# Decode attention with a gated MLP: w_in loaded first, and narrower streams in the last V group and the output projections

## Chip, cores and metric

One core of one Trainium2 chip. The metric is the device time of one execution in microseconds (us). A kernel's profile is one execution; its span, from the first to the last instruction, is about 2.0 us shorter than the measured time. In the names of groups, PE is TensorE's matrix multiply and PEld its weight load; DVE is VectorE, ACT is ScalarE, SP is the engine that issues the loads. In the tiles' names, uT is the vector that the gated MLP hands to w_out, and oa the attention output that goes to wo.

## The reference, cut to what matters

```python
q = x @ wq                      # x: [1, 1024], 32 heads of 128
k, v = k_cache, v_cache         # 4 groups x 65536 keys x 128, bf16; 8 heads share a group
a = softmax(q k^T / sqrt(128)) v @ wo
z = gelu(x @ w_in)              # w_in: [1024, 3584]
z1, z2 = halves of z;  z2 = layernorm(z2)
b = (z1 * (w_sp * z2 + b_sp)) @ w_out
out = g * a + (1 - g) * b       # g = sigmoid(sum(x * gate_w))
```

Everything is read once: 134 MB of K and V, 8.4 MB each of wq and wo, 7.3 MB of w_in, 3.7 MB of w_out, together 162.0 MB.

## The kernel before

All big loads go through one function into five buffers of 4 MB. SP issues them in program order, and each one waits until the buffer of the load five places earlier has been consumed.

```python
WO_SPLIT = (16, 8, 4, 2, 2)     # rows of wo for each partition, by load
W, WL = 64, 128
kv = ctx.enter_context(tc.tile_pool(name="kv", bufs=NKV))      # NKV = 5
def load(src, shape, name):
    t = kv.tile([P, CT * P], BF16, name=name, tag="kv")
    ...
    nc.sync.dma_start(out=v, in_=src)
```

The order is: wq and q; K of the four groups (each 128x128 block is transposed on PE, copied, and used as the stationary operand of the scores), with V of the group before interleaved; then w_in (z), alternating with the last group's V; then w_out and wo.

```python
# V: 8 columns are needed; the stream is padded to wv columns
wv = W if g + 1 < G else WL
nc.tensor.matmul(o_ps[g][:, o0:o0 + wv], lhsT=vt[:, c, :], rhs=scT[g][:, lo:hi, :]..., ...)
...
z_part(0); last_v(0); z_part(1); ...gelu, layernorm...; last_v(1..3)
...
# projections: one column is needed; it is broadcast to WL columns, NB = 4 to a tile, so there are two tiles
NB = 512 // WL
out_ps = [pss.tile([P, NB, WL], FP32, ...) for _ in range(NJ // NB)]
def project(src, n, vec, c0, name, first=False, last=False):
    w = load(src, (n, D), name)
    for c in range(n):
        for j in range(NJ):     # NJ = 8
            nc.tensor.matmul(out_ps[j // NB][:, j % NB, :], lhsT=w[:, c, j * P:(j + 1) * P],
                rhs=vec[:, c0 + c:c0 + c + 1].to_broadcast([P, WL]), ...)
project(w_out ...)              # 14 rows: 112 matmuls
for n in WO_SPLIT: project(wo_view[:, c0:c0 + n, :], n, oa, ...)   # 32 rows: 256 matmuls
# epilogue: copy out_ps, transpose, cast, store
```

Of the kernel before, what the change touches and what calls it, by code (L numbers as in the profile page):

```python
# [7 lines left out]
FP32 = mybir.dt.float32  # L8
BF16 = mybir.dt.bfloat16
I32 = mybir.dt.int32  # L10
ACT = mybir.ActivationFunctionType
ALU = mybir.AluOpType
AX = mybir.AxisListType

P = 128
# [3 lines left out]
CPS = 64  # L19
LAG = 4  # L20
EVAC_PAT = "vav"
WO_SPLIT = (16, 8, 4, 2, 2)
SW = 256
W = 64
WL = 128


@with_exitstack
def kernel(
# [15 lines left out]
    nc = tc.nc  # L45

    _, _, D = A_x.shape
    _, G, S, DH = A_k_cache.shape
# [3 lines left out]
    F = B_w_in.shape[1]  # L52
    FH = F // 2
    KC = D // P
    FC = FH // P
    OC = HD // P
    NJ = D // P
    QD = P // H
    NCG = S // P
    NT = NCG // CT  # L60
    SCALE = float(DH) ** -0.5
    assert DH == P and D % P == 0 and FH % P == 0 and P % H == 0
    assert S % (P * CT) == 0 and CT % CPS == 0 and CPS % TG == 0 and sum(WO_SPLIT) == OC

    const = ctx.enter_context(tc.tile_pool(name="const", bufs=1))
    wk = ctx.enter_context(tc.tile_pool(name="wk", bufs=2))
# [4 lines left out]
    pss = ctx.enter_context(tc.tile_pool(name="pss", bufs=2, space=bass.MemoryType.PSUM))  # L71
    psm = ctx.enter_context(tc.tile_pool(name="psm", bufs=1, space=bass.MemoryType.PSUM))
# [3 lines left out]
    def load(src, shape, name):  # L76
        t = kv.tile([P, CT * P], BF16, name=name, tag="kv")
        n = 1
        for s in shape:
            n *= s  # L80
        v = t[:, :n]
        if len(shape) == 2:
            v = v.rearrange("p (a b) -> p a b", b=shape[1])
        nc.sync.dma_start(out=v, in_=src)  # L84
        return v

    def load_kv(src, g, j, name):
# [9 lines left out]
    nc.scalar.dma_start(out=wb[:, 0:1], in_=B_w_sp)  # L97
    nc.scalar.dma_start(out=wb[:, 1:2], in_=B_b_sp.unsqueeze(0))

    wq_view = A_wq.rearrange("(p c) n -> p c n", c=KC)  # L100
    KH = KC // 2
    wq_t = [load(wq_view[:, i * KH:(i + 1) * KH, :], (KH, HD), "wq_t") for i in range(2)]


# [8 lines left out]
    ones_f = const.tile([P, P], FP32, name="ones_f")  # L113
# [4 lines left out]
                            op0=ALU.bitwise_and)  # L118
    nc.vector.tensor_scalar(out=pbits[:, 1:2], in0=pidx[:], scalar1=OC - 1, scalar2=None,
                            op0=ALU.bitwise_and)  # L120
    nc.vector.tensor_scalar(out=pbits[:, 2:3], in0=pidx[:], scalar1=OC.bit_length() - 1,
                            scalar2=None, op0=ALU.logical_shift_right)
# [4 lines left out]
    def one_hot(shape, dtype, in0, col, name):  # L127
# [17 lines left out]
                     start=True, stop=True)  # L145
    xm = const.tile([P, 2, KC, P // KC], FP32, name="xm")
    for t in range(2):
        nc.vector.tensor_tensor(
            out=xm[:, t], in0=xb_ps[:, t * P:(t + 1) * P].rearrange("p (i c) -> p c i", c=KC),
            in1=sel_i[:].unsqueeze(1).to_broadcast([P, KC, P // KC]), op=ALU.mult)  # L150
    xa = const.tile([P, 2, KC], FP32, name="xa")
    nc.vector.tensor_reduce(out=xa[:], in_=xm[:], axis=AX.X, op=ALU.add)
    xT = const.tile([P, KC], BF16, name="xT")
# [14 lines left out]
                            op0=ALU.add)  # L168
    nc.vector.reciprocal(out=gw[:, 2:3], in_=gw[:, 1:2])
    nc.vector.tensor_scalar(out=gw[:, 5:6], in0=gw[:, 2:3], scalar1=-1.0, scalar2=1.0,  # L170
                            op0=ALU.mult, op1=ALU.add)
    gate, wsp, bsp, gate1 = gw[:, 2:3], gw[:, 3:4], gw[:, 4:5], gw[:, 5:6]


    q_ps = psm.tile([P, H], FP32, name="q_ps", tag="m")
    for c in range(KC):
        w = wq_t[c // KH]
        for h in range(H):
            nc.tensor.matmul(  # L179
                q_ps[:, h:h + 1], lhsT=w[:, c % KH, h * DH:(h + 1) * DH], rhs=xT[:, c:c + 1],  # L180
                start=(c == 0 and h == 0), stop=(c == KC - 1), skip_group_check=True,
# [9 lines left out]
    scT, mxr, spt, o_ps, s_ps = {}, {}, {}, {}, {}  # L191
# [84 lines left out]
    def v_units(g, j, vt):  # L276
        wv = W if g + 1 < G else WL
        wc = wv // REP
# [53 lines left out]
    while steps:  # L332
        run_step()


    win_view = B_w_in.rearrange("(p c) n -> p c n", c=KC)
    zw = 512 // (2 * FC)
    z_ps = psm.tile([P, 2 * FC, zw], FP32, name="z_ps", tag="m")

    def z_part(i):  # L340
        t = load(win_view[:, i * KH:(i + 1) * KH, :], (KH, F), "win_t")
        for c in range(KH):
            w = t[:, c, :].rearrange("p (h m f) -> p h f m", h=2, f=FC)
            for hf in range(2):
                for f in range(FC):
                    nc.tensor.matmul(  # L346
                        z_ps[:, hf * FC + f, :], lhsT=w[:, hf, f, :],
                        rhs=xT[:, i * KH + c:i * KH + c + 1].to_broadcast([P, zw]),
                        start=(i == 0 and c == 0 and hf == 0 and f == 0),
                        stop=(i == 1 and c == KH - 1), skip_group_check=True)  # L350

    def last_v(j):
        rest(v_units(G - 1, j, load_kv(A_v_cache, G - 1, j, "vt")))

    z_part(0)
    last_v(0)
    z_part(1)
    z = wk.tile([P, 2 * FC], FP32, name="z")
    nc.vector.tensor_copy(out=z[:], in_=z_ps[:, :, 0])  # L359
    gt = wk.tile([P, 2 * FC], FP32, name="gt")  # L360
    nc.vector.tensor_tensor(out=gt[:], in0=z[:], in1=z[:], op=ALU.mult)
    nc.vector.tensor_scalar(out=gt[:], in0=gt[:], scalar1=0.044715, scalar2=1.0,
                            op0=ALU.mult, op1=ALU.add)
    nc.vector.tensor_tensor(out=gt[:], in0=gt[:], in1=z[:], op=ALU.mult)
    th = wk.tile([P, 2 * FC], FP32, name="th")
    nc.scalar.activation(out=th[:], in_=gt[:], func=ACT.Tanh, scale=0.7978845608028654)
    nc.vector.tensor_scalar(out=th[:], in0=th[:], scalar1=0.5, scalar2=0.5,
                            op0=ALU.mult, op1=ALU.add)
    zg = wk.tile([P, 2 * FC], FP32, name="zg")
    nc.vector.tensor_tensor(out=zg[:], in0=z[:], in1=th[:], op=ALU.mult)  # L370
    z2 = zg[:, FC:2 * FC]
    z2sq = wk.tile([P, FC], FP32, name="z2sq")
    nc.vector.tensor_tensor(out=z2sq[:], in0=z2, in1=z2, op=ALU.mult)
    rs = wk.tile([P, 2], FP32, name="rs")
    nc.vector.reduce_sum(out=rs[:, 0:1], in_=z2, axis=AX.X)
    nc.vector.reduce_sum(out=rs[:, 1:2], in_=z2sq[:], axis=AX.X)
    tot_ps = psm.tile([P, 2], FP32, name="tot_ps", tag="m")
    nc.tensor.matmul(tot_ps[:], lhsT=ones_f[:], rhs=rs[:], start=True, stop=True)
    stat = wk.tile([P, 8], FP32, name="stat")
    nc.vector.tensor_scalar(out=stat[:, 0:2], in0=tot_ps[:], scalar1=1.0 / float(FH),  # L380
                            scalar2=None, op0=ALU.mult)
    nc.vector.tensor_tensor(out=stat[:, 2:3], in0=stat[:, 0:1], in1=stat[:, 0:1], op=ALU.mult)
    nc.vector.tensor_tensor(out=stat[:, 3:4], in0=stat[:, 1:2], in1=stat[:, 2:3],
                            op=ALU.subtract)
    nc.vector.tensor_scalar(out=stat[:, 4:5], in0=stat[:, 3:4], scalar1=1e-5, scalar2=None,
                            op0=ALU.add)
    nc.scalar.activation(out=stat[:, 5:6], in_=stat[:, 4:5], func=ACT.Sqrt)
    nc.vector.reciprocal(out=stat[:, 6:7], in_=stat[:, 5:6])
    z2n = wk.tile([P, FC], FP32, name="z2n")
    nc.vector.tensor_scalar(out=z2n[:], in0=z2, scalar1=stat[:, 0:1], scalar2=stat[:, 6:7],  # L390
                            op0=ALU.subtract, op1=ALU.mult)
    nc.vector.tensor_scalar(out=z2n[:], in0=z2n[:], scalar1=wsp, scalar2=bsp,
                            op0=ALU.mult, op1=ALU.add)
    uT = const.tile([P, FC], BF16, name="uT")
    nc.vector.scalar_tensor_tensor(out=uT[:], in0=zg[:, 0:FC], scalar=gate1, in1=z2n[:],
                                   op0=ALU.mult, op1=ALU.mult)
    for j in range(1, NT):
        last_v(j)


    NB = 512 // WL
    out_ps = [pss.tile([P, NB, WL], FP32, name="out_ps", tag="spt") for _ in range(NJ // NB)]

    def project(src, n, vec, c0, name, first=False, last=False):
        w = load(src, (n, D), name)
        for c in range(n):
            for j in range(NJ):
                nc.tensor.matmul(  # L408
                    out_ps[j // NB][:, j % NB, :], lhsT=w[:, c, j * P:(j + 1) * P],
                    rhs=vec[:, c0 + c:c0 + c + 1].to_broadcast([P, WL]),  # L410
                    start=(first and c == 0 and j % NB == 0), stop=(last and c == n - 1),
                    skip_group_check=True)


# [2 lines left out]
                     rhs=ones_f[0:1, 0:1], start=True, stop=True, skip_group_check=True)  # L417
    nc.tensor.matmul(om_ps[:, :OC], lhsT=lm[:].rearrange("p h q -> p (h q)"), rhs=sel_c[:],
                     start=False, stop=True, skip_group_check=True)
# [4 lines left out]
                            op0=ALU.mult, op1=ALU.mult)  # L424
# [3 lines left out]
    c0 = 0  # L428
    for n in WO_SPLIT:
        project(wo_view[:, c0:c0 + n, :], n, oa, c0, "wo_t", last=(c0 + n == OC))  # L430
        c0 += n
    out_sb = const.tile([P, NJ], FP32, name="out_sb")
    for i, t in enumerate(out_ps):
        nc.vector.tensor_copy(out=out_sb[:, i * NB:(i + 1) * NB], in_=t[:, :, 0])  # L434
    outT_ps = psm.tile([NJ, P], FP32, name="outT_ps", tag="m")
    nc.tensor.transpose(outT_ps[:], out_sb[:], ident_f[:])
    outT = const.tile([NJ, P], BF16, name="outT")
# [4 lines left out]
    last = {}  # L442
# [37 lines left out]
```

## Time and profile before

| | before |
|---|---|
| time, median of 4 runs (before the prediction: 3 runs, 398.57) | 398.07 us (397.54 to 399.08) |
| span of the profiled run | 396.6 us |
| DMA rate over 20 to 370 us | 408 to 444 GB/s |
| first wo piece: landed; PE starts it | 377.9; 378.6 us |
| last wo piece landed; last projection matmul | 387.7; 393.6 us |

First the forty-slice view of the kernel before. Each digit is the busy share of a fortieth of the span in tenths; PEclk is the granted TensorE clock, DMA the busy share of the 16 DMA engines.

```profile
PE   0435999778788787878888688896987789799997
...
PEclk9999999999999999999999999999999977789999
DMA  8999999999999999999999999999999999999960
GB/s 357 435 423 421 425 444 433 431 423 422 428 423 408 426 414 438 426 421 416 428 440 433 431 423 422 433 425 440 433 419 430 428 431 428 438 433 423 416 259 7
```

The DMA engines are full from the second slice to the thirty-eighth. PE is full in slices 36 to 39, and it still works in the last two, when the DMA ends.

The same end by windows. The columns are the window, its length, busy time (and instruction count) of PE, PEld, DVE, ACT and POOL, then PEclk, DMA share and GB/s.

```profile
core 0: us, PE busy (x) PEld busy (x) DVE busy (x) ACT busy (x) POOL busy (x), PEclk, DMA share, GB/s
360.00:370.00 10.00, 10.00 (x178) 9.94 (x176) 0.00 (x0) 0.00 (x0) 0.00 (x0) 1.00 1.00 429
375.00:380.00 5.00, 5.00 (x90) 5.00 (x88) 0.00 (x0) 0.00 (x0) 0.00 (x0) 1.00 0.83 337
380.00:385.00 5.00, 5.00 (x91) 5.00 (x89) 0.00 (x0) 0.00 (x0) 0.00 (x0) 1.00 0.63 248
385.00:390.00 5.00, 5.00 (x90) 5.00 (x88) 0.00 (x0) 0.00 (x0) 0.00 (x0) 1.00 0.19 74
```

From 375 us on the DMA share falls while PE is busy all the time. A share of 0.63, then 0.19, is not a queue that ends at once: some of the sixteen engines end long before others. The landing events of this trace show it: a big load has sixteen of them (I read each as one engine's part), and of the last wo piece eight come by 382.3 us and eight from 386.0 to 387.7.

The timeline of the tail (start and duration in us, engine, source line, operation, output and inputs, count):

```profile
370.84 8.32 SPq L84 DMA_DIRECT2D wo_t<-in_A_wo_dram  x2
...
372.17 6.63 PE L408 MATMUL out_ps<-uT,wout_t 128*128 128x128 bf16 x112
...
378.63 14.96 PE L408 MATMUL out_ps<-oa,wo_t 128*128 128x128 bf16 x256
393.40 0.39 DVE L434 COPY out_sb<-out_ps 128x4 f32<-128x4 f32 x2 [20.52 <-PE out_ps L408]
...
394.47 0.36 SPq L439 DMA_DIRECT2D out_dram<-outT  x1
```

The 112 matmuls of w_out take 6.6 us and the 256 of wo 15.0 us, 58 ns each. The loads of wo and their time to landing:

```profile
L84 SPq DMA_DIRECT2D wo_t<-in_A_wo_dram x5: 327/328/334, 344.0 to 378.8; - x5
DMA to landing us min/median/max: 8.9/21.4/33.9
```

The median is the mean of the two ends, so two of the five landings are known; I read them as those of the first and the last piece. The first was issued at 344.0 and landed 33.9 us later, at 377.9; the last was issued at 378.8 and landed 8.9 us later, at 387.7. PE ends 5.9 us after that. The chain that ended last says the same by shares of the span: the first line by engine, the second by line of the program.

```profile
PE 71%; DMA 13%; issue 11%; ACT 3%; DVE 1%; SPq 0%; ACTq 0%
PE tps L264 27%; PE o_ps L297 18%; PE spt L243 14%; DMA kn<-in_A_k_cache_dram 13%; PE out_ps L408 5%; PE z_ps L346 3%; PE o_ps L286 2%; ACT ktt L267 1%; ACT scT L230 1%; ACT scT L249 1%; PE nb_ps L221 0%; DVE mxr L206 0%; DVE mxr L251 0%; SPq L84 0%; DVE mx L209 0%
```

### The profile page before, as it was taken

Reading aid. Unit: us, or ns where it says so; the run is one execution under the profiler, and the core shown is the slowest. Engines: PE = TensorE matmul, PEld = TensorE weight load, DVE = VectorE, ACT = ScalarE, POOL = GpSimd, SP = SyncE. Lnnn points to the kernel's source line nnn. Section 1 sums busy time; section 2 is a strip of 40 time slices with the busy share of each in tenths; the row PEclk is TensorE's granted clock in tenths of the full one; section 3 lists DMA queues with packets and bytes.
Section 4 is the critical chain, followed back from the end, with each engine's and each line's share of the span. In section 5 each row is a group of like instructions: output and inputs, shape, how many; then the busy total and the mean of one; then the engine's idle time right before and its main releaser. Section 6 shows DMA issues by size and latency. Waiting matters only on the chain.

```text
span 396.6 us, 14958 instructions
## 1 busy us (share of the span) xinstructions
PE 316.6 (80%) x7080; PEld 309.1 (78%) x7080; DVE 152.7 (38%) x297; ACT 121.1 (31%) x138; POOL 1.0 (0%) x9
## 2 busy tenths in 40 slices
PE   0435999778788787878888688896987789799997
PEld 0435989777788787777878687786977689799896
DVE  2002666649344444654334346643444420110100
ACT  1002555446433233436333233553333130100000
POOL 1000000000000000000000000000000000000000
PEclk9999999999999999999999999999999977789999
DMA  8999999999999999999999999999999999999960
GB/s 357 435 423 421 425 444 433 431 423 422 428 423 408 426 414 438 426 421 416 428 440 433 431 423 422 433 425 440 433 419 430 428 431 428 438 433 423 416 259 7
DMA packets 6161, 162.96 MB, mean 411 GB/s; under 512 B 724, under 2 KB 724, under 8 KB 980
## 3 DMA queue, kind: packets, MB, share of 16 engines
q1 hardware_dynamic: 6064, 162.01, 95.7%
q8 instruction: 55, 0.90, 0.8%
q14 instruction: 6, 0.05, 0.0%
q10 hardware_dynamic: 36, 0.00, 0.0%
HBM read 162.01 MB, written 0.00 MB: 409 GB/s over the span
## 4 chain that ended last, share of the span: by engine, by line
PE 71%; DMA 13%; issue 11%; ACT 3%; DVE 1%; SPq 0%; ACTq 0%
PE tps L264 27%; PE o_ps L297 18%; PE spt L243 14%; DMA kn<-in_A_k_cache_dram 13%; PE out_ps L408 5%; PE z_ps L346 3%; PE o_ps L286 2%; ACT ktt L267 1%; ACT scT L230 1%; ACT scT L249 1%; PE nb_ps L221 0%; DVE mxr L206 0%; DVE mxr L251 0%; SPq L84 0%; DVE mx L209 0%
## 5 line engine op out<-in xcount | busy, mean ns | idle before, releaser
L264 PE MATMUL tps<-ident_b,kn 128*128 128x128 bf16 x2048 | 160.2, 222 | 19.4 <-issue 10.4
L269 DVE COPY ktt<-tps 128x1024 bf16<-128x1024 bf16 x171 | 116.8, 690 | 122.4 <-PE tps L264 122.0
L264 PEld LDWEIGHTS <-kn 128*128 128x128 bf16 x2048 | 121.9, 99 | 20.7 <-issue 13.1
L267 ACT COPY ktt<-tps 128x1024 bf16<-128x1024 bf16 x85 | 85.9, 1012 | 157.8 <-PE tps L264 157.7
L297 PE MATMUL o_ps<-scT,vt 128*128 128x64 bf16 (+1 forms) x2048 | 110.4, 203 | 14.3 <-issue 14.3
L243 PE MATMUL spt<-qT,ktt 128*128 128x64 bf16 (+7 forms) x2048 | 102.9, 192 | 17.9 <-issue 16.5
L297 PEld LDWEIGHTS <-vt 128*128 128x128 bf16 x2048 | 94.9, 100 | 16.1 <-issue 15.2
L243 PEld LDWEIGHTS <-ktt 128*128 128x128 bf16 x2048 | 84.8, 98 | 20.6 <-issue 18.7
L249 ACT CAST scT<-spt 128x512 bf16<-128x512 f32 x32 | 18.9, 589 | 24.0 <-PE spt L243 14.1
L230 ACT ACTIVATE scT<-scT 128x1024 bf16<-128x1024 bf16 x16 | 16.4, 1058 | 7.5 <-DVE scT L226 7.5
L286 PE MATMUL o_ps<-scT,ones_b 128*128 128x256 bf16 x64 | 17.8, 279 | 0.4 <-DVE ssum L308 0.3
L251 DVE TENSOR_TENSOR mxr<-scT,mxr 128x512 bf16<-128x512 bf16 x24 | 10.2, 425 | 16.5 <-ACT scT L249 15.0
L346 PE MATMUL z_ps<-xT,win_t 128*128 128x18 bf16 x224 | 13.8, 206 | 1.5 <-issue 1.5
L408 PE MATMUL out_ps<-oa,wo_t 128*128 128x128 bf16 x256 | 15.0, 219 | 0.0
L408 PEld LDWEIGHTS <-wo_t 128*128 128x128 bf16 x256 | 14.8, 98 | 0.0
L346 PEld LDWEIGHTS <-win_t 128*128 128x128 bf16 x224 | 13.7, 161 | 1.5 <-issue 1.5
L179 PE MATMUL q_ps<-xT,wq_t 128*128 128x1 bf16 x256 | 7.1, 165 | 6.9 <-DMA wq_t<-in_A_wq_dram 6.4
L179 PEld LDWEIGHTS <-wq_t 128*128 128x128 bf16 x256 | 7.1, 104 | 7.0 <-DMA wq_t<-in_A_wq_dram 6.5
L226 DVE TENSOR_TENSOR scT<-scT,negm 128x1024 bf16<-128x1024 bf16 x16 | 10.7, 685 | 0.1
L359 DVE COPY z<-z_ps 128x28 f32<-128x28 f32 x1 | 0.2, 188 | 24.4 <-PE z_ps L346 24.4
L303 DVE TENSOR_TENSOR lm<-sel_q,o_ps 128x32 f32<-128x32 f32 x4 | 0.7, 182 | 22.1 <-PE o_ps L297 22.1
L434 DVE COPY out_sb<-out_ps 128x4 f32<-128x4 f32 x2 | 0.3, 162 | 20.6 <-PE out_ps L408 20.5
(85 smaller groups left out, 52.6 us busy)
## 6 DMA issues: line engine op xcount, KB each, us to landing
kn<-in_A_k_cache_dram SPq DMA_DIRECT2D x16, 4096.0 KB, 43.2
vt<-in_A_v_cache_dram SPq DMA_DIRECT2D x16, 4096.0 KB, 27.2
wq_t<-in_A_wq_dram SPq DMA_DIRECT2D x2, 4096.0 KB, 17.4
win_t<-in_B_w_in_dram SPq DMA_DIRECT2D x2, 3584.0 KB
wo_t<-in_A_wo_dram SPq DMA_DIRECT2D x1, 4096.0 KB, 33.9
wout_t<-in_B_w_out_dram SPq DMA_DIRECT2D x1, 3584.0 KB
wo_t<-in_A_wo_dram SPq DMA_DIRECT2D x1, 2048.0 KB
wo_t<-in_A_wo_dram SPq DMA_DIRECT2D x1, 1024.0 KB
```

The source lines that it names most:

```text
L179: nc.tensor.matmul(q_ps[:, h:h + 1], lhsT=w[:, c % KH, h * DH:(h + 1) * DH], rhs=xT[:, c:c + 1], start=(c == 0 and h == 0), stop=(c == KC ...
L226: nc.vector.tensor_tensor(out=blk, in0=blk, in1=negm[:].unsqueeze(1).to_broadcast([P, CT, REP]), op=ALU.add)
L230: nc.scalar.activation(out=blk, in_=blk, func=ACT.Exp, scale=SCALE)
L243: nc.tensor.matmul(spt[g][:, o:o + n], lhsT=ktt[:, j * P:(j + 1) * P], rhs=qT[:, g * REP:g * REP + n], start=True, stop=True, skip_group_c ...
L249: nc.scalar.copy(out=blk, in_=spt[g][:].rearrange("p (c h) -> p c h", h=REP))
L264: nc.tensor.transpose(tps[:, i * P:(i + 1) * P], kn[:, u * TG + i, :], ident_b[:])
L267: nc.scalar.copy(out=ktt[:], in_=tps[:])
L269: nc.vector.tensor_copy(out=ktt[:], in_=tps[:])
L286: nc.tensor.matmul(o_ps[g][:, 2 * WL:], lhsT=ones_b[:], rhs=scT[g][:, j * CT + c:j * CT + c + SW // REP, :].rearrange("p c h -> p (c h)"), ...
L297: nc.tensor.matmul(o_ps[g][:, o0:o0 + wv], lhsT=vt[:, c, :], rhs=scT[g][:, lo:hi, :].rearrange("p c h -> p (c h)"), start=False, stop=(cg ...
L346: nc.tensor.matmul(z_ps[:, hf * FC + f, :], lhsT=w[:, hf, f, :], rhs=xT[:, i * KH + c:i * KH + c + 1].to_broadcast([P, zw]), start=(i == 0 ...
L408: nc.tensor.matmul(out_ps[j // NB][:, j % NB, :], lhsT=w[:, c, j * P:(j + 1) * P], rhs=vec[:, c0 + c:c0 + c + 1].to_broadcast([P, WL]), st ...
```

## The change

The intent is to take the MLP's first product out of the crowded tail and to stream fewer useless columns there. Most lines of the diff are moved code; this is the core, with cuts marked.

```diff
-WO_SPLIT = (16, 8, 4, 2, 2)
+WO_SPLIT = (16, 8, 4, 2, 1, 1)
-WL = 128
+WL = 96
...
+    win_view = B_w_in.rearrange("(p c) n -> p c n", c=KC)
+    win_t = [load(win_view[:, i * KH:(i + 1) * KH, :], (KH, F), "win_t") for i in range(2)]
     wq_t = [load(wq_view[:, i * KH:(i + 1) * KH, :], (KH, HD), "wq_t") for i in range(2)]
... z, gelu, layernorm and uT are computed here, ahead of q; K and V follow as before ...
-    z_part(0)
-    last_v(0)
-    z_part(1)
-    ...
-    for j in range(1, NT):
-        last_v(j)
+    for j in range(NT):
+        rest(v_units(G - 1, j, load_kv(A_v_cache, G - 1, j, "vt")))
-    NB = 512 // WL
-    out_ps = [pss.tile([P, NB, WL], FP32, name="out_ps", tag="spt") for _ in range(NJ // NB)]
+    out_ps = pss.tile([P, NJ, W], FP32, name="out_ps", tag="spt")
...
-                    rhs=vec[:, c0 + c:c0 + c + 1].to_broadcast([P, WL]),
+                    rhs=vec[:, c0 + c:c0 + c + 1].to_broadcast([P, W]),
...
-    for i, t in enumerate(out_ps):
-        nc.vector.tensor_copy(out=out_sb[:, i * NB:(i + 1) * NB], in_=t[:, :, 0])
+    nc.vector.tensor_copy(out=out_sb[:], in_=out_ps[:, :, 0])
```

More of the change, by code (lines that the diff above doesn't have):

```diff
@@ L98 @@
     nc.scalar.dma_start(out=wb[:, 1:2], in_=B_b_sp.unsqueeze(0))
+    KH = KC // 2
+    win_view = B_w_in.rearrange("(p c) n -> p c n", c=KC)
+    win_t = [load(win_view[:, i * KH:(i + 1) * KH, :], (KH, F), "win_t") for i in range(2)]
     wq_view = A_wq.rearrange("(p c) n -> p c n", c=KC)
-    KH = KC // 2
     wq_t = [load(wq_view[:, i * KH:(i + 1) * KH, :], (KH, HD), "wq_t") for i in range(2)]
@@ L172, with z_part @@
     gate, wsp, bsp, gate1 = gw[:, 2:3], gw[:, 3:4], gw[:, 4:5], gw[:, 5:6]
+    zw = 512 // (2 * FC)
+    z_ps = psm.tile([P, 2 * FC, zw], FP32, name="z_ps", tag="m")
+    def z_part(i):
+        for c in range(KH):
+            w = win_t[i][:, c, :].rearrange("p (h m f) -> p h f m", h=2, f=FC)
+            for hf in range(2):
+                for f in range(FC):
+                    nc.tensor.matmul(
+                        z_ps[:, hf * FC + f, :], lhsT=w[:, hf, f, :],
+                        rhs=xT[:, i * KH + c:i * KH + c + 1].to_broadcast([P, zw]),
+                        start=(i == 0 and c == 0 and hf == 0 and f == 0),
+                        stop=(i == 1 and c == KH - 1), skip_group_check=True)
@@ new lines @@
+    z_part(0)
+    z_part(1)
+    z = wk.tile([P, 2 * FC], FP32, name="z")
+    nc.vector.tensor_copy(out=z[:], in_=z_ps[:, :, 0])
+    gt = wk.tile([P, 2 * FC], FP32, name="gt")
+    nc.vector.tensor_tensor(out=gt[:], in0=z[:], in1=z[:], op=ALU.mult)
+    nc.vector.tensor_scalar(out=gt[:], in0=gt[:], scalar1=0.044715, scalar2=1.0,
+                            op0=ALU.mult, op1=ALU.add)
+    nc.vector.tensor_tensor(out=gt[:], in0=gt[:], in1=z[:], op=ALU.mult)
+    th = wk.tile([P, 2 * FC], FP32, name="th")
@@ new lines @@
+    nc.scalar.activation(out=th[:], in_=gt[:], func=ACT.Tanh, scale=0.7978845608028654)
+    nc.vector.tensor_scalar(out=th[:], in0=th[:], scalar1=0.5, scalar2=0.5,
+                            op0=ALU.mult, op1=ALU.add)
+    zg = wk.tile([P, 2 * FC], FP32, name="zg")
+    nc.vector.tensor_tensor(out=zg[:], in0=z[:], in1=th[:], op=ALU.mult)
+    z2 = zg[:, FC:2 * FC]
+    z2sq = wk.tile([P, FC], FP32, name="z2sq")
+    nc.vector.tensor_tensor(out=z2sq[:], in0=z2, in1=z2, op=ALU.mult)
+    rs = wk.tile([P, 2], FP32, name="rs")
@@ new lines @@
+    nc.vector.reduce_sum(out=rs[:, 0:1], in_=z2, axis=AX.X)
+    nc.vector.reduce_sum(out=rs[:, 1:2], in_=z2sq[:], axis=AX.X)
+    tot_ps = psm.tile([P, 2], FP32, name="tot_ps", tag="m")
+    nc.tensor.matmul(tot_ps[:], lhsT=ones_f[:], rhs=rs[:], start=True, stop=True)
+    stat = wk.tile([P, 8], FP32, name="stat")
+    nc.vector.tensor_scalar(out=stat[:, 0:2], in0=tot_ps[:], scalar1=1.0 / float(FH),
+                            scalar2=None, op0=ALU.mult)
+    nc.vector.tensor_tensor(out=stat[:, 2:3], in0=stat[:, 0:1], in1=stat[:, 0:1], op=ALU.mult)
@@ new lines @@
+    nc.vector.tensor_tensor(out=stat[:, 3:4], in0=stat[:, 1:2], in1=stat[:, 2:3],
+                            op=ALU.subtract)
+    nc.vector.tensor_scalar(out=stat[:, 4:5], in0=stat[:, 3:4], scalar1=1e-5, scalar2=None,
+                            op0=ALU.add)
+    nc.scalar.activation(out=stat[:, 5:6], in_=stat[:, 4:5], func=ACT.Sqrt)
+    nc.vector.reciprocal(out=stat[:, 6:7], in_=stat[:, 5:6])
+    z2n = wk.tile([P, FC], FP32, name="z2n")
+    nc.vector.tensor_scalar(out=z2n[:], in0=z2, scalar1=stat[:, 0:1], scalar2=stat[:, 6:7],
+                            op0=ALU.subtract, op1=ALU.mult)
@@ L175 @@
+    nc.vector.tensor_scalar(out=z2n[:], in0=z2n[:], scalar1=wsp, scalar2=bsp,
+                            op0=ALU.mult, op1=ALU.add)
+    uT = const.tile([P, FC], BF16, name="uT")
+    nc.vector.scalar_tensor_tensor(out=uT[:], in0=zg[:, 0:FC], scalar=gate1, in1=z2n[:],
+                                   op0=ALU.mult, op1=ALU.mult)
     q_ps = psm.tile([P, H], FP32, name="q_ps", tag="m")
@@ L333 @@
         run_step()
-    win_view = B_w_in.rearrange("(p c) n -> p c n", c=KC)
-    zw = 512 // (2 * FC)
-    z_ps = psm.tile([P, 2 * FC, zw], FP32, name="z_ps", tag="m")
-    def z_part(i):
-        t = load(win_view[:, i * KH:(i + 1) * KH, :], (KH, F), "win_t")
-        for c in range(KH):
-            w = t[:, c, :].rearrange("p (h m f) -> p h f m", h=2, f=FC)
-            for hf in range(2):
-                for f in range(FC):
-                    nc.tensor.matmul(
-                        z_ps[:, hf * FC + f, :], lhsT=w[:, hf, f, :],
-                        rhs=xT[:, i * KH + c:i * KH + c + 1].to_broadcast([P, zw]),
-                        start=(i == 0 and c == 0 and hf == 0 and f == 0),
-                        stop=(i == 1 and c == KH - 1), skip_group_check=True)
@@ L352, in last_v @@
-    def last_v(j):
-        rest(v_units(G - 1, j, load_kv(A_v_cache, G - 1, j, "vt")))
-    z_part(0)
-    last_v(0)
-    z_part(1)
-    z = wk.tile([P, 2 * FC], FP32, name="z")
-    nc.vector.tensor_copy(out=z[:], in_=z_ps[:, :, 0])
-    gt = wk.tile([P, 2 * FC], FP32, name="gt")
-    nc.vector.tensor_tensor(out=gt[:], in0=z[:], in1=z[:], op=ALU.mult)
-    nc.vector.tensor_scalar(out=gt[:], in0=gt[:], scalar1=0.044715, scalar2=1.0,
-                            op0=ALU.mult, op1=ALU.add)
-    nc.vector.tensor_tensor(out=gt[:], in0=gt[:], in1=z[:], op=ALU.mult)
@@ L365 @@
-    th = wk.tile([P, 2 * FC], FP32, name="th")
-    nc.scalar.activation(out=th[:], in_=gt[:], func=ACT.Tanh, scale=0.7978845608028654)
-    nc.vector.tensor_scalar(out=th[:], in0=th[:], scalar1=0.5, scalar2=0.5,
-                            op0=ALU.mult, op1=ALU.add)
-    zg = wk.tile([P, 2 * FC], FP32, name="zg")
-    nc.vector.tensor_tensor(out=zg[:], in0=z[:], in1=th[:], op=ALU.mult)
-    z2 = zg[:, FC:2 * FC]
-    z2sq = wk.tile([P, FC], FP32, name="z2sq")
-    nc.vector.tensor_tensor(out=z2sq[:], in0=z2, in1=z2, op=ALU.mult)
@@ L374 @@
-    rs = wk.tile([P, 2], FP32, name="rs")
-    nc.vector.reduce_sum(out=rs[:, 0:1], in_=z2, axis=AX.X)
-    nc.vector.reduce_sum(out=rs[:, 1:2], in_=z2sq[:], axis=AX.X)
-    tot_ps = psm.tile([P, 2], FP32, name="tot_ps", tag="m")
-    nc.tensor.matmul(tot_ps[:], lhsT=ones_f[:], rhs=rs[:], start=True, stop=True)
-    stat = wk.tile([P, 8], FP32, name="stat")
-    nc.vector.tensor_scalar(out=stat[:, 0:2], in0=tot_ps[:], scalar1=1.0 / float(FH),
-                            scalar2=None, op0=ALU.mult)
@@ L382 @@
-    nc.vector.tensor_tensor(out=stat[:, 2:3], in0=stat[:, 0:1], in1=stat[:, 0:1], op=ALU.mult)
-    nc.vector.tensor_tensor(out=stat[:, 3:4], in0=stat[:, 1:2], in1=stat[:, 2:3],
-                            op=ALU.subtract)
-    nc.vector.tensor_scalar(out=stat[:, 4:5], in0=stat[:, 3:4], scalar1=1e-5, scalar2=None,
-                            op0=ALU.add)
-    nc.scalar.activation(out=stat[:, 5:6], in_=stat[:, 4:5], func=ACT.Sqrt)
-    nc.vector.reciprocal(out=stat[:, 6:7], in_=stat[:, 5:6])
-    z2n = wk.tile([P, FC], FP32, name="z2n")
@@ L390 @@
-    nc.vector.tensor_scalar(out=z2n[:], in0=z2, scalar1=stat[:, 0:1], scalar2=stat[:, 6:7],
-                            op0=ALU.subtract, op1=ALU.mult)
-    nc.vector.tensor_scalar(out=z2n[:], in0=z2n[:], scalar1=wsp, scalar2=bsp,
-                            op0=ALU.mult, op1=ALU.add)
-    uT = const.tile([P, FC], BF16, name="uT")
-    nc.vector.scalar_tensor_tensor(out=uT[:], in0=zg[:, 0:FC], scalar=gate1, in1=z2n[:],
-                                   op0=ALU.mult, op1=ALU.mult)
-    for j in range(1, NT):
-        last_v(j)
@@ L408, in project @@
                 nc.tensor.matmul(
-                    out_ps[j // NB][:, j % NB, :], lhsT=w[:, c, j * P:(j + 1) * P],
-                    rhs=vec[:, c0 + c:c0 + c + 1].to_broadcast([P, WL]),
-                    start=(first and c == 0 and j % NB == 0), stop=(last and c == n - 1),
+                    out_ps[:, j, :], lhsT=w[:, c, j * P:(j + 1) * P],
+                    rhs=vec[:, c0 + c:c0 + c + 1].to_broadcast([P, W]),
+                    start=(first and c == 0 and j == 0), stop=(last and c == n - 1),
                     skip_group_check=True)
```

## The prediction

> **What bounds the kernel now.** The DMA queue, until its last twenty microseconds; then TensorE. The forty-slice view shows the DMA engines full (408 to 444 GB/s) until about 377 us. The tail by windows: DMA share 1.00 at 360-370 us, 0.83 at 375-380, 0.63 at 380-385, 0.19 at 385-390, while PE is 100% busy from 350 to 393 us. The chain that ended last runs, from 346 us on, through PE: last group's V, then 368 projection matmuls to 393.6 us (21.3 us, 58 ns each). By issue times and times to landing, the first wo piece landed at 377.9 (PE starts it at 378.6), the last, issued at 378.8, at 387.7. PE works 5.7 us past that, and 3.2 us of epilogue follow.
>
> One-microsecond windows show a DMA share of 0.46 to 0.53 from 382 to 386 us: half the engines finish late. In the packet records a 32 KB packet takes 1213 ns and 55 instruction packets of about 0.94 us stretch the others by 62 us in sum; if half of the 16 engines carry them, those are 7.8 us behind. [...] The slow half is never short of work before 387 us.
>
> **What the change does.** Bytes (162.0 MB) and instructions are the same, so the last landing should stay near 387.7 us. That is the floor.
> - w_in first: 17.1 us of loads move to the front; z (two times 6.8 us) runs there, where PE waits for DMA anyway. K starts about 17 us later (33.7 to about 51), the last K lands near 310 instead of 292.6. Worth nothing on the queue, but it takes 13.7 us of z and about 5 us of half-clock out of the PE-bound tail.
> - V at 96: a matmul falls from 56 to an estimated 43 ns (64 columns took 29), so a 4 MB V takes about 6 us against 9.8 us of transfer. PE catches up and waits.
> - Projections at 64: an estimated 29 ns warm, 55 cold; 368 fall from 21.3 to 11-15 us, mostly hidden. One eviction copy (0.2 us) goes.
> - wo's last piece halved: about 0.3 us.
>
> PE's waits of 3 to 5 us before late pieces may halve the clock ([...]here the clock returned 2.8 to 5.5 us after dense work resumed). I expect that to cost at most 1 us at the end: wo's first piece has 10 us before the last landing.
>
> **Time.** Last landing about 387.8, last matmul 388.3, epilogue 3.0: span 391.3 against 396.6. The measured time is 2.0 above the span: 393.3 us, 1.3% faster. Eight in ten: 391.3 to 396.0. Faster by over 2%: 0.07; within 2%: 0.91; slower: 0.02.
>
> **What would show it.** Right: last wo landing at 387 to 388.5; PE waits for DMA before V, wout and wo; the chain ends with DMA, not 21 us of PE; z near 12-30 us. Wrong: PE cold throughout wo (+3 us); the last piece issued too late, since it waits for wo's first piece to be consumed; fewer instruction packets, or other engines carrying them, and so an earlier landing; DMA starving when the last K is consumed.

The sum: 387.8 for the last landing, 388.3 for the last matmul and 3.0 of epilogue, a span of 391.3 us, and 393.3 with 2.0 more. The 55 ns "cold" is shown by the kernel before: 64-column matmuls start 53 to 54 ns apart from 107.1 to 110.5 us, where the clock is at half, and 29 ns apart at full clock. The 62 us is the sum of what packets took above the median of their size. That instruction packets caused it was my assumption: of the 104 packets of 32 KB that took over 0.1 us more than the median, 57 overlap an instruction packet in time.

## The result

The kernel after took 393.38 us (median of 4 runs, 392.85 to 393.89) against 398.07 (397.54 to 399.08). The ratio is 0.9879, with a 95% interval of 0.9852 to 0.9906: 1.2% faster. Ratios here are the mean time of one kernel's fast runs over that of the other's of the same rounds, so not quite the ratio of the medians. Executions over 1.5% slower than the fastest of the same kernel are left out of the means.

The slices after:

```profile
PE   0774379977889789868897878887986877887947
...
PEclk9999999999999989999999999999999999998979
DMA  8999999999999999999999999999999999999983
GB/s 329 432 434 435 437 429 433 430 430 425 430 426 430 422 424 415 410 432 434 432 429 430 422 434 432 424 425 435 427 433 434 432 423 429 427 424 428 424 352 119
```

PE now has gaps in the tail as well, and of the last two slices the DMA has 8 and 3 tenths instead of 6 and 0, mostly because the span now ends 5 us earlier and the loads do not. By windows:

```profile
core 0: us, PE busy (x) PEld busy (x) DVE busy (x) ACT busy (x) POOL busy (x), PEclk, DMA share, GB/s
360.00:370.00 10.00, 9.16 (x174) 8.92 (x175) 1.16 (x5) 0.00 (x0) 0.00 (x0) 0.84 1.00 427
375.00:380.00 5.00, 1.76 (x34) 1.76 (x35) 0.00 (x0) 0.00 (x0) 0.00 (x0) 0.68 0.85 359
380.00:385.00 5.00, 5.00 (x116) 5.00 (x114) 0.00 (x0) 0.00 (x0) 0.00 (x0) 0.63 0.48 196
385.00:390.00 5.00, 3.90 (x118) 3.58 (x114) 0.45 (x2) 0.00 (x0) 0.00 (x0) 1.00 0.31 105
```

PE is busy for 1.76 of the 5 us from 375 to 380: it waits. The clock is at 0.68 and then 0.63 there. The DMA share from 380 to 385 is 0.48, about half. The tail:

```profile
368.79 3.65 PE L403 MATMUL out_ps<-uT,wout_t 128*128 128x64 bf16 x112
...
378.24 10.38 PE L403 MATMUL out_ps<-oa,wo_t 128*128 128x64 bf16 x256 [5.80 <-DMA wo_t<-in_A_wo_dram]
388.66 0.17 DVE L428 COPY out_sb<-out_ps 128x8 f32<-128x8 f32 x1 [19.15 <-PE out_ps L403]
...
389.50 0.36 SPq L433 DMA_DIRECT2D out_dram<-outT  x1
```

The 256 matmuls of wo take 10.4 us instead of 15.0, and they start at 378.2, hardly earlier than before (378.6). This start is a landing:

```profile
L84 SPq DMA_DIRECT2D wo_t<-in_A_wo_dram x6: 327/328/335, 344.4 to 384.7; - x6
...
  DMA wo_t<-in_A_wo_dram: 11.7, 2
...
DMA to landing us min/median/max: 3.3/14.9/33.8
```

The first wo piece, issued at 344.4, landed 33.8 us later, at 378.2. The last, issued at 384.7, landed at 387.9 (387.93 by the trace's landing events). In the kernel before these were 377.9 and 387.7. So the change moved neither of these landings to speak of (0.3 us later, both), and took 5 us off what PE does after them: it ends 0.7 us past the last landing instead of 5.9. The chain:

```profile
PE 62%; DMA 21%; issue 11%; ACT 3%; DVE 1%; SPq 0%; ACTq 0%
PE tps L322 30%; PE spt L301 15%; DMA kn<-in_A_k_cache_dram 12%; PE o_ps L355 12%; DMA wo_t<-in_A_wo_dram 9%; PE out_ps L403 3%; ACT scT L288 2%; PE o_ps L344 1%; ACT ktt L325 1%; ACT scT L307 1%; SPq L84 0%; PE nb_ps L279 0%; DVE mxr L264 0%; ACTq L469 0%; DVE mxr L309 0%
```

The load of wo is in it now, with 9% of the span, and PE's projections fell from 5% to 3%. The end of the chain in order of time:

```profile
344.43 33.77 DMA wo_t<-in_A_wo_dram
...
378.24 10.39 PE out_ps L403 x256
```

It runs through the landing of wo's first piece, not of the last. PE works without a pause from 378.2 to 388.6 us, at half clock until 383.7 (granted clock 0.50 from 378 to 382), and it comes to the last piece's 8 matmuls at 388.2, 0.3 us after that piece has landed. So two limits end almost together here: the last landing, and PE's work behind the first landing.

### The profile page after: what moved, and what is told of

Its sections match the earlier page's. It is cut to its first block, busy times and chain, and to the rows that moved or that the text cites. A ratio compares the mean times of both kernels' runs of the same rounds, so it can differ in the third digit from the quotient of the medians.

```text
span 391.5 us, 14960 instructions
## 1 busy us (share of the span) xinstructions
PE 301.1 (77%) x7080; PEld 291.4 (74%) x7080; DVE 152.3 (39%) x296; ACT 122.4 (31%) x139; POOL 1.0 (0%) x9
## 4 chain that ended last, share of the span: by engine, by line
PE 62%; DMA 21%; issue 11%; ACT 3%; DVE 1%; SPq 0%; ACTq 0%
PE tps L322 30%; PE spt L301 15%; DMA kn<-in_A_k_cache_dram 12%; PE o_ps L355 12%; DMA wo_t<-in_A_wo_dram 9%; PE out_ps L403 3%; ACT scT L288 2%; PE o_ps L344 1%; ACT ktt L325 1%; ACT scT L307 1%; SPq L84 0%; PE nb_ps L279 0%; DVE mxr L264 0%; ACTq L469 0%; DVE mxr L309 0%
## 5 line engine op out<-in xcount | busy, mean ns | idle before, releaser
L355 PE MATMUL o_ps<-scT,vt 128*128 128x64 bf16 (+1 forms) x2048 | 102.3, 198 | 17.1 <-issue 14.8
L301 PE MATMUL spt<-qT,ktt 128*128 128x64 bf16 (+7 forms) x2048 | 101.8, 192 | 15.1 <-issue 13.1
L355 PEld LDWEIGHTS <-vt 128*128 128x128 bf16 x2048 | 86.2, 99 | 20.0 <-issue 16.6
L309 DVE TENSOR_TENSOR mxr<-scT,mxr 128x512 bf16<-128x512 bf16 x24 | 10.2, 425 | 15.8 <-ACT scT L307 14.3
L403 PE MATMUL out_ps<-oa,wo_t 128*128 128x64 bf16 x256 | 10.4, 212 | 5.8 <-DMA wo_t<-in_A_wo_dram 5.8
L403 PEld LDWEIGHTS <-wo_t 128*128 128x128 bf16 x256 | 10.3, 111 | 5.9 <-DMA wo_t<-in_A_wo_dram 5.9
L185 PE MATMUL z_ps<-xT,win_t 128*128 128x18 bf16 x224 | 13.7, 209 | 1.0 <-DMA win_t<-in_B_w_in_dram 0.6
L185 PEld LDWEIGHTS <-win_t 128*128 128x128 bf16 x224 | 13.7, 158 | 1.1 <-DMA win_t<-in_B_w_in_dram 0.7
L284 DVE TENSOR_TENSOR scT<-scT,negm 128x1024 bf16<-128x1024 bf16 x16 | 10.7, 685 | 0.1
L344 PEld LDWEIGHTS <-ones_b 128*128 128x128 bf16 x64 | 6.3, 99 | 2.5 <-issue 1.6
## 6 DMA issues: line engine op xcount, KB each, us to landing
wo_t<-in_A_wo_dram SPq DMA_DIRECT2D x1, 4096.0 KB, 33.8
```

The costliest lines, as they stand in the source:

```text
L185: nc.tensor.matmul(z_ps[:, hf * FC + f, :], lhsT=w[:, hf, f, :], rhs=xT[:, i * KH + c:i * KH + c + 1].to_broadcast([P, zw]), start=(i == 0 ...
L284: nc.vector.tensor_tensor(out=blk, in0=blk, in1=negm[:].unsqueeze(1).to_broadcast([P, CT, REP]), op=ALU.add)
L301: nc.tensor.matmul(spt[g][:, o:o + n], lhsT=ktt[:, j * P:(j + 1) * P], rhs=qT[:, g * REP:g * REP + n], start=True, stop=True, skip_group_c ...
L344: nc.tensor.matmul(o_ps[g][:, 2 * WL:], lhsT=ones_b[:], rhs=scT[g][:, j * CT + c:j * CT + c + SW // REP, :].rearrange("p c h -> p (c h)"), ...
L403: nc.tensor.matmul(out_ps[:, j, :], lhsT=w[:, c, j * P:(j + 1) * P], rhs=vec[:, c0 + c:c0 + c + 1].to_broadcast([P, W]), start=(first and ...
```

## Experiments

Comments behind # in the diffs below are mine. The theory after the result: the time ends with the landing of wo plus whatever PE has left to do, and PE's leftover was the width of the projections. Rivals: the order did it (z and its half clock left the tail; in the kernel before the clock is at half from 322.1 to 332.4 and from 342.6 to 349.5 us), or V at 96 did it. The first four kernels went together, on one chip, with the kernel before at 398.46 us (median of 8) beside them.

### Order alone

```diff
 # the kernel after, with
-WO_SPLIT = (16, 8, 4, 2, 1, 1)
+WO_SPLIT = (16, 8, 4, 2, 2)
-WL = 96
+WL = 128
 # and the projections in two banks at 128 columns, as before
```

> Only the order of the change: w_in loaded and used first, V at 128 columns, projections at 128 columns in two banks, w_o pieces 16,8,4,2,2. Theory (the gain is the narrower projections; the order is worth nothing alone): the first w_o piece still lands near 378 us and 256 projection matmuls at 58 ns (first ones slower if the clock has halved) end near 393 us or later: span 396.4 to 399, time 398.4 to 401, ratio to before 1.00 to 1.006. Rival (taking z's 13.7 us and its half clock out of the PE-bound tail gives the gain): time 393 to 394.5, ratio 0.988.

Measured 397.98 us (397.9 to 399.3), ratio 1.0001 (0.9968 to 1.0033). The order alone is worth nothing (the time is 0.4 us below the range that I expected). The end of its chain (start and duration in us):

```profile
344.89 32.98 DMA wo_t<-in_A_wo_dram
...
377.91 14.99 PE out_ps L404 x256
```

The first wo piece lands at 377.9 as ever, and 256 matmuls at 58 ns follow it.

### Projections alone

```diff
 # the kernel before, with
-    out_ps = [pss.tile([P, NB, WL], ...) for _ in range(NJ // NB)]
+    out_ps = pss.tile([P, NJ, W], FP32, name="out_ps", tag="spt")
 # the matmuls at W = 64 columns, and one copy instead of two
```

> The kernel before with one edit: projections stream 64 columns into one bank; z stays in the tail, V at 128, w_o pieces 16,8,4,2,2. Theory: last landing stays at 387.7 us, last matmul near 388.3, span 391.2, time 393.2, ratio 0.988: the whole gain. Rival (order gives the gain): time 396 to 398, ratio 0.995 to 1.0.

Measured 392.85 us (392.84 to 393.43), ratio 0.9866 (0.9838 to 0.9894), span 391.0. This edit of a few lines is the whole gain; moved w_in, V at 96 and the sixth wo piece add nothing that shows. The end of its chain:

```profile
340.94 36.66 DMA wo_t<-in_A_wo_dram
...
377.64 9.71 PE out_ps L407 x240
...
387.36 0.68 PE out_ps L407 x16
```

PE reaches the last piece's 16 matmuls at 387.4 (issued at 373.8 and 13.5 us to landing, so landed near 387.3) and ends 0.7 us later.

### All but the projections

```diff
 # the kernel after, with the projections at 128 columns in two banks
```

> The kernel after with its projections put back to 128 columns in two banks; w_in first, V at 96, w_o pieces 16,8,4,2,1,1 stay. Theory: the PE waits nearly 6 us for the first w_o piece, starts it at half clock (107 ns a matmul for 3 to 5 us), then 58 ns: last matmul 394 to 395.5, span 397 to 398.5, time 399 to 400.5, ratio 1.002 to 1.006, so the change without this part loses. Rival: time near 394, ratio 0.99.

Measured 397.79 us (397.69 to 399.53), ratio 0.9999 (0.9964 to 1.0035). Without this part the change gains nothing, as the theory has it. The size that I expected was wrong by about 2 us: I had counted on half clock in the first wo piece, and in this kernel V and w_out kept PE busy so long that it waited only 1.5 us for that piece and the clock was full from 375 us on (1.00 in all windows to 393). The 107 ns are the step of 128-column matmuls at half clock in the kernel before, from 346.7 to 349.4 us.

### V back to 128 columns

```diff
 # the kernel after, with
-WL = 96
+WL = 128
```

> The kernel after with the last group's V put back to 128 columns. Theory: the V stream still ends near 368 us, before w_out lands, so nothing at the end moves: span 391.5, time 393.4, ratio 0.988. Rival (V at 96 matters: it lets the PE catch up): V ends 2 us or more later, w_o starts later than 378.3 us, time 394.5 or more.

Measured 393.27 us (392.79 to 395.59), ratio 0.9869 (0.9841 to 0.9897). V's width is worth nothing in this tail. (The profiled run is the one of 395.59; its wo landed over 1 us later than in the others, so I draw nothing from its trace.)

### Fewer PE instructions

What sets the landing near 388 us? The DMA share of one half in the last microseconds (0.43 from 386 to 388 us) says that about eight of the sixteen engines end late; in the kernel after, eight landings of wo's first piece come by 371.2 us and eight from 376.1 on. PE's program is 7080 matmuls and 7080 weight loads, and the profile shows 55 instruction packets with 0.90 MB (16384 bytes each in the packet records), one for 257 of these 14160 instructions:

```profile
q8 instruction: 55, 0.90, 0.8%
```

That these packets fetch PE's instructions, and that they are what delays some engines, was my guess. The experiment takes instructions out and leaves all loads in:

```diff
-            for i in range(TG):
+            for i in range(TG) if g + 1 == G else (TG - 1,):     # one V matmul of 8 in groups 0 to 2
```

> The kernel after, wrong on purpose: groups 0 to 2 issue one V matmul of every eight, which takes out 1344 matmuls and their weight loads[...]; all loads stay. Theory (half of the DMA engines finish late because they also fetch PE's instructions, about 1.13 us of one engine's time a block): instruction packets fall from 55 to 44 or 45, the sum by which data packets are stretched from 61 to about 50 us, and the slow half finishes 11 x 1.13 / 8 = 1.5 us earlier; span 390.0, time 391.9. Rival (these engines are slow of themselves, or HBM is): packets fall, but the last landing stays and the span is 391.5.

(A block there is one instruction packet; its 1.13 us is 62 us over 55 packets. By the 257 of above, 2688 instructions are an estimated 10.5.)

Measured 391.6 us (391.24 to 392.17), span 389.7; ratio to before 0.9837 (0.982 to 0.9854). Its output is wrong, which doesn't matter for the time. Its packets, and its last windows beside the window of the kernel after:

```profile
q8 instruction: 45, 0.74, 0.7%
```

```profile
384.00:386.00 2.00, 2.00 (x70) 2.00 (x67) 0.00 (x0) 0.00 (x0) 0.00 (x0) 1.00 0.43 138
386.00:388.00 2.00, 1.04 (x26) 0.72 (x22) 0.45 (x2) 0.00 (x0) 0.00 (x0) 1.00 0.03 8
```

```profile
386.00:388.00 2.00, 2.00 (x71) 2.00 (x68) 0.00 (x0) 0.00 (x0) 0.00 (x0) 1.00 0.43 158
```

From 386 to 388 us the kernel after still moves 158 GB/s; here the loads are over. The first wo piece lands at 376.2 instead of 378.2. A sharper mark is the 1 MB piece of wo (8 KB a packet) in the trace's packet records. Its last packet ends at

```
before 384.8   after 385.1   order alone 384.8   projections alone 384.5
all but the projections 384.8   after, run again 384.9   fewer instructions 383.0
```

These six traces with 55 packets lie within 0.6 us; with 45 packets it is 1.5 to 2.1 us earlier, against 1.5 expected. Three more with 55 packets are not in the list: 384.7 with wo's first piece halved, 386.0 with the probe loads, 387.4 in the V-at-128 trace that I set aside; none is earlier.

The run took matmuls away with the instructions, and so PE freed buffers sooner: wo's first piece was issued at 338.1 us instead of 344.4. Is that the cause, and not the fetch? The landing events speak against it. Those of wo's first piece come in two groups of eight. In the run with the projections alone the early eight land at 367.7 us in the mean and the late eight at 376.8; with fewer instructions the early eight land at 367.8, no sooner, and the late eight at 375.0. And the lag of the late ones grows in steps. In the kernel after, the last of a 4 MB load's sixteen landings comes 9.5 to 10.1 us after that of the load before, but 10.7 to 11.1 us at 91.0, 150.4, 200.5, 250.3, 300.1 and 350.0 us: mostly 50 us apart, and there eight instruction packets take 50 to 53 us. With fewer instructions the long steps come at 90.5, 150.2, 219.4, 288.6 and 357.9 us, mostly 69 us apart, and from 150 us on eight packets take 65 to 78 us. So the steps of the lag come at the pace of the instruction packets. No run changes these packets alone, so how much of the 2 us is due to PE's other work stays open. (The comparison with the reference is blind to most of V.) One part of my figure was not sound: the sum by which data packets are stretched, from which I had 1.13 us a block, ranged from 40 to 75 us among kernels with the same 55 packets and loads at the usual rate.

### A piece of wo in loads of eight partitions

```diff
+        if split:                       # the piece of four rows, 1 MB
+            for p in range(0, P, 8):
+                nc.sync.dma_start(out=v[p:p + 8], in_=src[p:p + 8])
```

> The kernel after, with the 1 MB piece of w_o (four rows a partition) loaded by 16 transfers of 8 partitions instead of one of 128. [...] Theory (eight fixed engines end late)[...] Rival (the late engines are not a fixed low or high half, or the DMA is bound by HBM in all): no move beyond 0.5 us.

The theory came to a span of 389.0 us (ratio 0.981) or of 394, depending on which eight engines are late; it rested on an assumption about which engines such a load runs on, and no run shows that. Measured 401.18 us (400.22 to 405.0), ratio 1.0092 (1.0055 to 1.0128): slower, and for a reason that neither side had. SP's waits from 340 us on:

```profile
SPq L86 <- DMA wo_t<-in_A_wo_dram: 15.1, 2, 10.1
...
SPq L86 <- DMA wout_t<-in_B_w_out_dram: 8.2, 1, 8.2
```

SP issued five of the sixteen small loads by 360 us and then waited for earlier loads to land, 8.2, 10.1 and 5.0 us, before the next ones. The trace has load completions on eight semaphores only; that the small loads had used them up is my reading. So the test of the theory was spoiled. The landing events of the small loads were of use, though: of the eight data landings of the first such load, six came at 374.1 to 375.7 us and two at 382.9 to 383.1. So the eight landings of one small load were not all early or all late.

### Small loads behind wo's first piece

```diff
+        if n == 16:                     # behind wo's first piece
+            for k in (2, 4, 6, 10, 12, 14):
+                pr = const.tile([k, 256], BF16, name=f"probe{k}")
+                nc.sync.dma_start(out=pr[:], in_=A_wo[0:k, 0:256])
```

> A measurement of the disputed thing by itself, time not of interest: the kernel after, with six tiny unused loads of 2, 4, 6, 10, 12 and 14 partitions (one row of 512 B each) queued right behind w_o's first piece[...]. Theory (a fixed eight engines lag by 7 to 8 us[...]): each load's landings fall into two clumps 6 to 8 us apart, the late clump [...]at most two for n up to 8 and growing to eight at 16. Rival (lag moves about): counts that do not grow with n, or a smear without clumps. Span 392 to 398.

One run of unknown state, 394.28 us. The trace has n data landings for a probe of n partitions. They fall into two clumps:

```
partitions       2   4   6   8*  10  12  14
early (by 371)   2   4   5   6   7   7   7
late (over 376)  0   0   1   2   3   5   7      * from the run with 8-partition loads; early by 375.7, late at 383
```

The clumps are 5.7 us or more apart. wo's first piece, just before them, has sixteen: in this trace eight come by 369.9 us and eight from 375.9 us on. The late count grows from 0 at 2 and 4 partitions to 7 at 14, as the theory had it. Which engine a landing belongs to the trace does not say, so which engines are late, and whether they are a fixed set, was not shown.

### Sixteen partitions in loads of four

```diff
+        if low4:                        # second half of w_in, and w_out
+            for p in range(0, 16, 4):
+                nc.sync.dma_start(out=v[p:p + 4], in_=src[p:p + 4])
+            nc.sync.dma_start(out=v[16:], in_=src[16:])
```

> The kernel after, same bytes in all: w_in's second half and w_out are each loaded with their first 16 partitions as four transfers of 4 partitions[...] and the other 112 partitions as one transfer. [...] Theory (the landing waits for the late eight engines): w_o's first piece lands near 376.1 instead of 378.2, the last piece near 386, span 389.4 against 391.5, time 391.3; against the unchanged kernel after in the same call 0.5% faster. Rival (total rate or queue depth bounds the landing): no gain, or a loss from the extra transfers, span 391.5 or more.

What is cut is the assumption that the small loads run on early engines, which no run shows, and the term that rested on it: an estimated 2.1 us less for each late engine. Measured 425.93 us (425.16 to 427.03), ratio 1.0711 (1.0687 to 1.0735). My expectation, 391.3 us, missed by 35 us. The windows at the front, where w_in is split:

```profile
10.00:20.00 10.00, 7.43 (x115) 7.37 (x114) 0.70 (x5) 0.17 (x1) 0.00 (x0) 1.00 0.99 181
20.00:30.00 10.00, 0.00 (x0) 0.00 (x0) 0.00 (x0) 0.00 (x0) 0.00 (x0) 1.00 0.96 177
30.00:40.00 10.00, 0.00 (x0) 0.00 (x0) 0.00 (x0) 0.00 (x0) 0.00 (x0) 1.00 0.91 216
40.00:50.00 10.00, 6.86 (x112) 6.80 (x112) 1.46 (x9) 1.03 (x2) 0.00 (x0) 1.00 1.03 441
```

For some thirty microseconds the engines count as busy (0.91 to 0.99) and move 177 to 216 GB/s, less than half of the usual; the same follows at w_out (209 to 260 GB/s in slices 36 to 38). A packet of 28 KB takes 1.06 us in an ordinary load (median in the kernel after); here the median was 2.9 us until the last 4-partition load had landed (26.9 us), and 2.1 us for the rest of the 112-partition load. So packets took two to three times as long in these loads. Why was not shown: no run separates the causes.

> The same with 16 matmuls of 512 columns[...] between w_out and w_o, so that the clock is full when w_o's first piece lands. Theory: a further 0.3 to 0.8 us, since the first piece is consumed and the last piece issued sooner: span 388.8, time 390.7. Rival: as e9_balance within 0.2 us.

The same with 16 of the filler matmuls of the next experiment: 424.6 us (424.26 to 425.72), ratio 1.0681 (1.0661 to 1.07). That is 1.3 us less than without them, but the ranges touch. The two traces show what the filler does. Without it the clock is at half from 408.8 to 415.7 us, and the first 128 matmuls of wo take 6.4 us; with it the clock is full, they take 4.2 us, and PE then waits for the last landing. From the landing of wo's first piece to the last matmul it is 10.2 us instead of 10.5: the full clock is worth 0.3 us, since the last landing takes over. The rest of the difference is that the first piece landed 0.8 us sooner.

### A full clock for wo

```diff
+    for _ in range(NWARM):              # NWARM = 24, between w_out and wo
+        nc.tensor.matmul(warm_ps[:], lhsT=ones_b[:], rhs=scT[G - 1][:, :CPS, :]..., ...)
```

> The kernel after, with 24 matmuls of 512 columns[...] into an unused bank between the w_out and the w_o projections, where PE waits for w_o's first piece. Theory: the clock stays full, the first piece's 128 matmuls take 3.8 us instead of 6.5, so its buffer comes free about 2.5 us earlier and the last piece is issued at 382 instead of 384.7; last landing 387.4, last matmul 387.8 instead of 388.6: span 390.7, 0.8 us less. Rival (the end is the slow engines' landing alone, the clock hides behind it): 0 to 0.3 us.

Three runs took 392.73 to 393.11 us, ratio 0.9869 (0.985 to 0.9887). A fourth took 501.58 us with a mean clock of 0.60: the slow state, put aside, and as the profile fell in it there is no trace to compare. The kernel after, run again on another chip, took 393.13. By the times that is a gain of 0.2 us (fast medians 392.89 and 393.13); by the ratios to the kernel before it is 0.8 us (0.9869 against 0.9889, with intervals that overlap). So these runs neither show the 0.8 us nor exclude it; the two traces of the experiment before this one speak for the rival.

### The kernel after again, and a smaller first piece of wo

> The kernel after, unchanged, for comparison on the same chip in the same rounds: 393.4 us, ratio to before 0.988.

Measured 393.13 us (392.94 to 393.62), ratio 0.9889 (0.9872 to 0.9905), span 391.1.

```diff
-WO_SPLIT = (16, 8, 4, 2, 1, 1)
+WO_SPLIT = (8, 8, 8, 4, 2, 1, 1)
```

> The kernel after with w_o's first piece halved: pieces of 8, 8, 8, 4, 2, 1, 1 rows instead of 16, 8, 4, 2, 1, 1. Theory (the landing near 387.2 is set by the late engines; the last 0.8 to 1.4 us after it are PE's half clock in the 16-row piece and the last piece waiting for that piece's buffer): the first 8 rows land near 373.3, PE starts w_o 5 us sooner, the last piece is issued near 380 instead of 384.7 and lands near 387.2, the last matmul ends 387.7 instead of 388.6: span 390.5, time 392.4, ratio to before 0.986. Rival (only the landing counts and it stays): span 391.1 to 391.5, ratio 0.988 to 0.989.

Three runs took 392.90 to 393.17 us, span 391.0 (a slow one took 401.24); ratio to a kernel before that ran at 398.86: 0.9857 (0.9826 to 0.9888). The end of its chain:

```profile
381.32 6.24 DMA wo_t<-in_A_wo_dram
...
387.61 0.43 PE out_ps L403 x8
```

PE now waits for the last landing (387.6) and does 8 matmuls after it. Yet the time is that of the kernel after: the landing is the floor, and what PE's half clock had cost at the end (last matmul at 388.6 us there, at 388.0 here) is within the scatter of the runs. No version that I ran correctly beats the kernel after beyond doubt; the one with the projections alone equals it.

## Why the prediction was right

- **What bounds the end.** I put the floor at the last landing, near 387.8 us, and said that bytes and instructions do not change. It came at 387.9. Shown by both traces, and by the fewer-instructions run, which moved the floor and the time together. One mark of mine failed: the chain was to end with the last landing, and in the kernel after it ends with 10.4 us of PE behind the landing of wo's first piece. That the two limits fell within 0.3 us of each other is partly luck; in the run with a halved first piece PE does wait for the last landing.
- **Order worth nothing.** Predicted for the DMA queue, and true for the time: 1.0001 alone. z ran from 13 to 27 us, K started at 51.0, the last K landed at 310.0. But I also credited the move with taking 13.7 us out of a PE-bound tail; alone that bought nothing. The loads of K and V moved back by the same 17 us, so PE came out of w_out only 3 us sooner (375.6 instead of 378.6), and of that 2.3 us became a wait for wo's first piece.
- **V at 96.** 46 ns a matmul against 43 expected (32 weight loads in 1.48 us), 6.1 us for the third 4 MB. PE then waited for V (2.2 us) and for wo (5.8 us), as predicted; the predicted wait for w_out did not come (it landed at 368.5, PE began on it at 368.8). Worth nothing, by its own run.
- **Projections at 64.** w_out's 112 took 3.65 us instead of 6.63, wo's 256 took 10.4 instead of 15.0. This is the gain: 0.9866 alone, 0.9999 for the rest.
- **Half clock.** Predicted at most 1 us. The first 128 wo matmuls took 6.2 us, 49 ns each, after PE had been idle for 5.8 us: it stopped at 372.4 us, and the granted clock was at half from 376.8 to 383.7. In the runs with a wait of 1.5 us (all but the projections) and 2.3 us (order alone) the clock was full under wo; with 3.9 us (projections alone) it was at half from 376 to 382 us, as here. It delayed the last issue to 384.7, since SP waited for the first piece's buffer (the longest of two waits below, 6.4 us):

```profile
SPq L84 <- PE out_ps L403: 10.3, 2, 6.4
```

  The last matmul ended at 388.64 against 388.3 predicted, the epilogue took 2.9 us against 3.0, and the span was 391.5 against 391.3.
- **Weak spot.** The 7.8 us by which half of the engines lag was reasoned from 62 us of stretched packets. The lag is there (in the kernel after, the late eight landings of wo's first piece come 7.4 us after the early eight in the mean, in the kernel before 6.8), but that sum was shown to be no steady measure. Two small slips stand in the prediction: from 370 to 375 us PE was busy for 4.2 of the 5 us, not all of it, and it ended 5.9 us past the last landing, not 5.7.

## What to carry to other kernels

When a kernel is full on DMA and its tail is full on PE, cost the PE work that follows the late landings, not the PE work of the tail. What stood before a landing turned into waiting when it was cut (PE waited 5.8 us for wo's first piece); here only the 256 matmuls behind wo's landing counted, and halving their columns gave all of the gain. Then ask what sets the landing itself: here the DMA share dropped to one half at the end (0.48 from 380 to 385 us) and eight of sixteen landings were late (by 7.4 us in the mean), and 2688 fewer PE instructions went with a landing 2 us sooner (wo's first piece at 376.2 instead of 378.2), where fewer matmul columns had left it in place (377.6 with the projections alone).
